# Four indirect transfers under way at most, and rows before weights in the 256-token lists

## The chip, the core and the metric

The kernel runs on one core of one Trainium2 chip. The metric is the device time of one execution in microseconds. Before the change it was 1098.66 us, the median of three runs (1090.99, 1098.66, 1099.57). Five engines work side by side and wait for each other through semaphores: TensorE (PE in the profile; PEld is its weight load), VectorE (DVE), ScalarE (ACT), GpSimd (POOL) and SyncE (SP). In this kernel SP only issues plain and transposing DMAs, and POOL almost only issues indirect ones.

## What is computed

The input `x` has 8 batches of 2496 tokens with 256 channels. A two-dimensional Fourier transform is taken over tokens and channels of each batch and its real part kept. Each of the 19,968 resulting rows then goes through one of 8 experts:

```python
x = np.fft.fft(np.fft.fft(x, axis=1), axis=2).real      # per batch
logits = x @ w_gate + modality_bias[modality_id]
e_idx = np.argmax(logits, axis=1)
gate_w = softmax(logits)[arange(N), e_idx]
for e in range(8):
    mask = e_idx == e
    out[mask] = gate_w[mask, None] * (np.maximum(x[mask] @ w1[e], 0) @ w2[e])
```

`w1[e]` is 256 x 1024 and `w2[e]` is 1024 x 256.

## The kernel before, in words

**Two programs in one.** The stream `Kernel.stream` makes the transform, batch after batch, as matmuls in three stages (lines 517/519, 543 to 552 and 561/563), and routes each batch: for each of its rows it finds the expert and the place in that expert's region of the DRAM buffer `xd`. The expert part `Kernel.block` takes 128 or 256 rows of one expert out of `xd` and runs both layers on them. A driver (`fft_moe`) interleaves the two by the string `SEQ` and later by due times; a scheduler then fixes, when the program is built, the order on every engine from its own idea of when things finish.

**Values are split.** Each fp32 value is held as two fp16 halves, so that a product takes three matmuls (line 1130 for the first layer, L1148 for the second). Before the experts run, the weights are read, split and written to `w16` (lines 881 to 928).

**Scatters.** A batch's rows are written to `xd` by 22 indirect DMAs of GpSimd (`scatter`, L744), each of up to 117 rows of 1032 bytes, from tiles `rp` and `rm`. The next tile `rm` is filled by DVE (L218 to L221) when an earlier scatter from its buffer has landed. There are 3 `rm` buffers early on.

**A block** (`block`). SP reads the block's first row, its expert and a flag from a small table (lines 1101 to 1105, `TENSOR_LOAD`); loads the expert's weights `w1` and `w2` (L1108, L1109; 1 MB each, skipped where the flag says that the slot has them already; three slots); fetches the rows transposed as `xT` (L1114, three buffers); and fetches `ig`, each row's token number and gate (L1117, four buffers). PE makes the first layer (L1130), ACT and DVE bring it out of PSUM as two halves of `H` (L1135, L1136), PE makes the second layer into the only `pso` buffer (L1148), DVE computes the row factor `gs` from `ig` (L1151), ACT scales `pso` into `ob` (L1154, two buffers, one of 128 rows each), and GpSimd writes `ob` to the output rows that `ig` names (L1155, indirect). So a 256-row block has two `ob` and two output transfers.

**Lists.** The first 19 blocks follow a fixed plan, with sizes 128 and 256. Then come six lists of 256-row blocks, one after batch 2 and one after every later batch (5, 10, 9, 10, 10 and 10 blocks), and at the end a list of 128-row blocks.

**Who is kept apart from whom.** Dependences between DMAs that write the same DRAM tensor are declared away: scatters belong to the group `xd_w` and declare no dependence on that group (`scatter_dep`), output transfers do the same with the group `out_w` (L1158, L1159).

**Queues.** SP issues its DMAs in program order: one that waits holds all that stand behind it. So does POOL. The indirect DMAs of POOL take eight completion counters in turn (`DMASW0` to `DMASW7`), and each waits until the transfer that had its counter before, the eighth before it, has landed.

Of the kernel before, what the change touches and what calls it, by code (L numbers as in the profile page):

```python
# [24 lines left out]
E, F = 8, 1024  # L25
# [30 lines left out]
WROW = 8208  # L56
# [34 lines left out]
CUT = 6  # L91
LAG = 1
SM = 3
HA = 0
GROUPS = {0: (1, (128,) * 3 + (0,) * 5), 1: (2, (128,) * 3 + (256,) * 3 + (0,) * 2),
          2: (3, (256,) * 8), 3: (3, (0,) * 6 + (256,) * 2)}
# [140 lines left out]
class Kernel:  # L237
    def __init__(self, ctx, tc, t):
        self.ctx, self.tc, self.nc, self.t = ctx, tc, tc.nc, t
        nc = self.nc  # L240
        pool = lambda name, bufs=1, **k: ctx.enter_context(tc.tile_pool(name=name, bufs=bufs, **k))
        self.cpool = c = pool("consts")
        self.fft = pool("fft", 2)
        self.rt = pool("route", 2)
        self.psf = pool("psf", 4, space=PSUM)
        self.psm = pool("psm", 3, space=PSUM)
        self.pso = pool("pso", 1, space=PSUM)
        self.pool = pool

        self.ready = -1  # L250
        self.parts = 0
        self.head = None
        self.XM = [None, None]

        def const(name, shape, dt=F32):
            x = c.tile(shape, dt, name=name)
            nc.sync.dma_start(x, t["c_" + name])
            return x

        self.load_x(0, 0, 0)  # L260
        self.c1 = c.tile([P, NI, 132], F32, name="c1")
        nc.sync.dma_start(self.c1[:, 0:NH], t["c_c1"][:, 0:NH])
        self.load_x(0, 0, 1)
        if XE:
            self.load_x(0, 1, 0)
            nc.sync.dma_start(self.c1[:, NH:NI], t["c_c1"][:, NH:NI])
            self.load_x(0, 1, 1)
            pk = const("pack", [P, PACK])
        else:
            pk = const("pack", [P, PACK])  # L270
            self.load_x(0, 1, 0)
            nc.sync.dma_start(self.c1[:, NH:NI], t["c_c1"][:, NH:NI])
            self.load_x(0, 1, 1)
        self.mp = pk[:, 0:512].rearrange("p (a c) -> p a c", a=4)
        self.misc = pk[:, 512:584]
        self.pk = pk
        self.wg = pk[:, 584:616].rearrange("p (a c) -> p a c", a=4)
        self.e3 = pk[0:120, 616:616 + 2 * M3].rearrange("p (a c) -> p a c", a=2)
        self.iota = pk[:, 850:978]
        self.ids = const("ids", [M3, B, NC], I32)  # L280
        self.tri = const("tri", [M3, 2, P], F16)
        self.mb = c.tile([P, 2, 8], F32, name="mb")
        nc.sync.dma_start(self.mb, t["mb"].unsqueeze(0).to_broadcast([P, 2, 8]))

        self.ones = c.tile([P, P], F32, name="ones")
        nc.vector.memset(self.ones, 1.0)
        self.base = c.tile([P, 8], F32, name="base")
        nc.vector.tensor_copy(self.base, self.misc[:, 16:24])
        pad = c.tile([P, ROW], I16, name="padrow")
        nc.gpsimd.memset(pad, 0)  # L290
        padi = pad.bitcast(I32)
        nc.gpsimd.memset(padi[:, 256:257], OOB)
        self.padrow = pad
        for i in range(2):
            self.scatter_dep(nc.sync.dma_start(t["xd"][DUMP + i * P: DUMP + (i + 1) * P, :], pad), 0)
        self.done = c.tile([1, 8], F32, name="done0")
        nc.vector.memset(self.done, 0.0)
        self.ntok = 0
        self.extra = 0
        self.ntaken = 0  # L300
        self.nblk = 0
        self.loads = []
        self.pend = []
        self.rows = None
        self.started = False
        self.prev = None
        self.ob = None
        self.off = 0
        self.mark = None
        self.bases = {}  # L310
        self.pos = 0.0
        self.slots = lambda b: 2 * NC
# [430 lines left out]
    def scatter(self, row, at, b):  # L743
        i = self.nc.gpsimd.indirect_dma_start(  # L744
            out=self.t["xd"], out_offset=bass.IndirectOffsetOnAxis(ap=at, axis=0),
            in_=row, in_offset=None, bounds_check=XROWS - 1, oob_is_err=False)
        self.scatter_dep(i, b)
        self.scattered = i.ins

    def drain(self, last):  # L750

# [33 lines left out]
    def stream(self):  # L785
# [13 lines left out]
        for b in range(B):  # L799
# [5 lines left out]
            for g, _ in enumerate(self.stage23(b)):  # L805
# [9 lines left out]
                if b == 0 and g == CUT + LAG - 1:  # L815
                    early = self.route(0, 0, CUT)
                with self.hp(HA):
                    next(early, None)
# [40 lines left out]
    def weights(self, p):  # L859
        U = 2 * E  # L860
        tc = self.tc
        L, A = {}, {}
        for s in range(U + 3):
            if 0 <= s - 3 < U:
                self.wstore(s - 3)
            if s < U:
                L[s] = self.wload(p, s)
            if 0 <= s - LA < U:
                with self.hp(HW), ExitStack() as x:
                    if PS <= s - LA < PS + 2:  # L870
                        x.enter_context(tc.issue_after(self.scattered))
                    A[s - LA] = self.wbound(p, s - LA, L[s - LA])
            if 0 <= s - LA - LB < U:
                with self.hp(HW):
                    self.wsplit(p, s - LA - LB, *A.pop(s - LA - LB))
            yield
# [58 lines left out]
    def first_taken(self):  # L935
        rt, V = self.rt, self.nc.vector
        nd = rt.tile([1, 8], F32, name="sp_d", bufs=2)
        V.memset(nd[:, SM:E], 0.0)
        V.tensor_tensor(nd[:, 0:SM], self.bases[1][0:1, 0:SM], self.misc[0:1, 16:16 + SM], ALU.subtract)
        V.tensor_scalar(nd[:, 0:SM], nd[:, 0:SM], float(P), None, ALU.min)  # L940
        self.done = nd
        self.ntaken += P * SM
        self.extra += SM

# [138 lines left out]
    def block(self, S, ti, i, o=0, n=0, ex=None, load=False, here=False, slot=0):  # L1083

        nc, t, p, tc = self.nc, self.t, self.mo, self.tc
# [4 lines left out]
        first = i < ns  # L1090
        if ex is None:
            w = i % ns
            i = o + sum((n - j + ns - 1) // ns for j in range(w)) + i // ns
        self.nblk += 1
        w1, w2 = self.w1[sl], self.w2[sl]
        kw = {}
        with ExitStack() as st:
# [4 lines left out]
            if ex is None:  # L1102
                ee = nc.sync.value_load(ti[0:1, 1, i:i + 1], min_val=0, max_val=E - 1)
                if not first:
                    kw = dict(cond=nc.sync.value_load(ti[0:1, 2, i:i + 1], min_val=0, max_val=1), cond_hint=False)
        if ex is None or load:
            wsrc = t["w16"][ds(ee, 1)].rearrange("a p f -> (a p) f") if ex is None else t["w16"][ex]
            nc.sync.dma_start(w1, wsrc[:, 0:4 * F], **kw)  # L1108
            nc.sync.dma_start(w2, wsrc[:, 4 * F:WROW], **kw)  # L1109
        if here:  # L1110
            xT, ig = self.onchip(ex)
        else:
            xT = p.tile([P, 4, S], I16, name=f"xT{S}", tag="xT", bufs=3)
            r1 = nc.sync.dma_start_transpose(xT, t["xd"][ds(ro, S), 0:512])  # L1114
            xT = xT.bitcast(F16)
            ig = p.tile([P, NT, 2], F32, name=f"ig{S}", bufs=4)
            r2 = nc.sync.dma_start(ig.bitcast(I16), t["xd"][ds(ro, S), 512:516].rearrange("(t p) c -> p t c", p=P))  # L1117
            self.loads.append(r2.ins)
            self.gather_dep(r1.ins)
            self.gather_dep(r2.ins)  # L1120
        H = p.tile([P, 2, 8, S], F16, name=f"H{S}", tag="H", bufs=2)
        w1v = w1.rearrange("p (h k f) -> p h k f", h=2, k=2)
        NF = 512 // S
        for f0 in range(0, 8, NF):
# [7 lines left out]
            with ExitStack() as st:  # L1132
                if self.ob is not None:
                    st.enter_context(tc.issue_after(self.ob))
                nc.scalar.activation(H[:, 0, f0:f0 + NF, :], ps, AF.Relu)  # L1135
            self.mark = V.scalar_tensor_tensor(H[:, 1, f0:f0 + NF, :], ps, 0.0, H[:, 0, f0:f0 + NF, :], ALU.max, ALU.subtract).ins  # L1136
        self.l1 = l1
# [3 lines left out]
        for tg in range(NT):  # L1141
            k = 0
            for ft in range(8):
                for hh, wh in ((0, 0), (0, 1), (1, 0)):
                    with ExitStack() as st:
                        if S == P and k == 0:
                            st.enter_context(tc.issue_after(self.l1))
                        nc.tensor.matmul(po[:, tg, :], H[:, hh, ft, tg * P:(tg + 1) * P], w2v[:, wh, ft, :], start=k == 0, stop=k == 23)  # L1148
                    k += 1
        gs = p.tile([P, NT], F32, name=f"gs{S}", bufs=3)  # L1150
        V.tensor_scalar(gs, ig[:, :, 1], w2[:, 4 * F:4 * F + 2].bitcast(F32), None, ALU.mult)  # L1151
        for tg in range(NT):
            ob = p.tile([P, D], F32, name="ob", bufs=2)
            self.ob = nc.scalar.activation(ob, po[:, tg, :], AF.Identity, scale=gs[:, tg:tg + 1]).ins  # L1154
            ins = nc.gpsimd.indirect_dma_start(  # L1155
                out=t["out"], out_offset=bass.IndirectOffsetOnAxis(ap=ig.bitcast(I32)[:, tg, 0:1], axis=0),
                in_=ob, in_offset=None, bounds_check=TOK - 1, oob_is_err=False).ins
            tc.declare_no_dep(ins, group="out_w", reason="rows are disjoint")  # L1158
            tc.add_to_no_dep_group("out_w", ins)  # L1159
            if self.started:  # L1160
                self.trickle(ins)
        yield
# [162 lines left out]
```

## Time and profile before

| | before |
|---|---|
| median of the three runs shown | 1098.66 us |
| the profiled execution: device time | 1105.77 us |
| the profiled execution: span of the profile | 1103.9 us |
| PE busy | 1022.9 us |
| POOL busy | 377.4 us |
| DVE, ACT busy | 562.4 us, 442.5 us |
| mean granted TensorE clock | 0.974 |
| mean DMA rate | 213 GB/s |

The span begins at the first instruction and ends with the last; 1.9 us of the device time lie outside it. The profiled execution is 7.1 us longer than the median of the runs. "Busy" adds up the time in which an engine works on at least one instruction. In a row such as `PE psm L1130 <- DVE H L1136` the engine to the left sat idle until the one to the right had finished what stands there; "issue" is idle time for which the profile shows no other engine.

### The profile page before, as it was taken

Reading aid. Unit: us, or ns where it says so; the run is one execution under the profiler, and the core shown is the slowest. Engines: PE = TensorE matmul, PEld = TensorE weight load, DVE = VectorE, ACT = ScalarE, POOL = GpSimd, SP = SyncE. Lnnn points to the kernel's source line nnn. Section 1 sums busy time; section 2 is a strip of 40 time slices with the busy share of each in tenths; the row PEclk is TensorE's granted clock in tenths of the full one; section 3 lists DMA queues with packets and bytes.
Section 4 is the critical chain, followed back from the end, with each engine's and each line's share of the span. In section 5 each row is a group of like instructions: output and inputs, shape, how many; then the busy total and the mean of one; then the engine's idle time right before and its main releaser. Section 6 shows DMA issues by size and latency. Waiting matters only on the chain.

```text
span 1103.9 us, 26274 instructions
## 1 busy us (share of the span) xinstructions
PE 1022.9 (93%) x10069; PEld 916.4 (83%) x10069; DVE 562.4 (51%) x1672; ACT 442.5 (40%) x886; POOL 377.4 (34%) x351
## 2 busy tenths in 40 slices
PE   6789978998897889999999999999999999999996
PEld 5687867987787778989888989887788888889995
DVE  4988866866686565764456434742223222222221
ACT  5667656534434334433343333232223323222331
POOL 0265185134342434324432332344534212211111
PEclk9899988999998899999999999999999999999998
DMA  9388866598377585584966584489678988394963
GB/s 353 150 304 321 264 229 221 159 237 249 128 217 234 184 266 178 148 261 139 287 205 177 163 254 128 111 281 254 191 204 276 261 255 240 95 294 127 267 181 45
DMA packets 151586, 235.56 MB, mean 213 GB/s; under 512 B 115772, under 2 KB 118725, under 8 KB 133533
## 3 DMA queue, kind: packets, MB, share of 16 engines
q1 hardware_dynamic: 132077, 191.65, 59.9%
q0 software_dynamic: 19376, 42.16, 10.8%
q8 instruction: 81, 1.33, 0.5%
q14 instruction: 52, 0.43, 0.1%
HBM read 204.27 MB, written 60.48 MB: 240 GB/s over the span
## 4 chain that ended last, share of the span: by engine, by line
PE 63%; issue 14%; DMA 9%; DVE 4%; POOL 4%; ACT 3%; SPq 2%; another core or an unknown queue 0%; POOLq 0%; DVEq 0%; ACTq 0%
PE pso L1148 28%; PE psm L1130 28%; DMA XM<-x 2%; POOL out L1155 2%; PE psf L561 2%; PE psf L543 2%; POOL xd L744 2%; DMA wa<-w 2%; SPq L1114 2%; DMA out<-ob,ig 1%; PE psf L517 1%; DMA xd<-rm,dsti 1%; ACT wj L896 1%; DMA ig<-xd 1%; DMA c<-c_c 1%
## 5 line engine op out<-in xcount | busy, mean ns | idle before, releaser
L1130 PE MATMUL psm<-xT,w 128*128 128x256 f16 (+1 forms) x4512 | 462.2, 258 | 24.1 <-issue 10.4
L1148 PE MATMUL pso<-w,H 128*128 128x256 f16 x3864 | 459.0, 275 | 11.4 <-issue 10.2
L1130 PEld LDWEIGHTS <-w 128*128 128x128 f16 x4512 | 387.7, 98 | 65.8 <-issue 27.6
L1148 PEld LDWEIGHTS <-H 128*128 128x128 f16 x3864 | 378.0, 99 | 63.0 <-issue 18.3
L1136 DVE SCALAR_TENSOR_TENSOR H<-psm,H 128x512 f16<-128x512 f32 x322 | 218.7, 686 | 298.3 <-ACT H L1135 236.4
L1155 POOL DMA_INDIRECT out<-ob,ig x161 | 162.4, 1009 | 594.2 <-ACT ob L1154 563.0
L1135 ACT ACTIVATE H<-psm 128x512 f16<-128x512 f32 x322 | 189.0, 598 | 298.3 <-PE psm L1130 205.3
L1154 ACT ACTIVATE ob<-pso,gs 128x256 f32<-128x256 f32 x161 | 69.5, 470 | 235.7 <-PE pso L1148 171.8
L744 POOL DMA_INDIRECT xd<-rp,dsti x88 | 102.6, 1166 | 91.2 <-issue 75.3
L744 POOL DMA_INDIRECT xd<-rm,dsti x88 | 103.8, 1180 | 30.7 <-issue 24.1
L498 DVE SCALAR_TENSOR_TENSOR T<-psf,T 120x280 f16<-120x280 f32 (+2 forms) x95 | 43.5, 463 | 56.3 <-ACT T L497 46.4
L1151 DVE TENSOR_SCALAR gs<-ig,w 128x2 f32<-128x2 f32 (+1 forms) x94 | 21.3, 227 | 81.8 <-DMA ig<-xd 65.6
L497 ACT ACTIVATE T<-psf 120x280 f16<-120x280 f32 (+2 forms) x95 | 39.4, 426 | 18.1 <-PE psf L543 8.5
L561 PE MATMUL psf<-T,pack 120*117 120x145 f16 x330 | 35.0, 227 | 9.5 <-DVE T L498 5.3
L896 ACT ACTIVATE wj<-wa 128x1024 f16<-128x1024 f32 x32 | 34.1, 1064 | 15.2 <-DMA wa<-w 15.0
L561 PEld LDWEIGHTS <-pack 120*117 120x117 f16 x330 | 29.2, 135 | 8.8 <-issue 7.7
L379 DVE TENSOR_TENSOR XM<-XM 128x1280 f32<-128x1280 f32 (+2 forms) x18 | 24.1, 1339 | 20.6 <-DMA XM<-x 20.6
L543 PE MATMUL psf<-pack,T 128*120 128x144 f16 x330 | 33.2, 233 | 0.3 <-issue 0.3
L922 DVE SCALAR_TENSOR_TENSOR w<-wa,wsc,w 128x1024 f16<-128x1024 f32 (+1 forms) x16 | 28.9, 1809 | 2.0 <-ACT w L921 1.9
L921 ACT ACTIVATE w<-wa,wsc 128x1024 f16<-128x1024 f32 (+1 forms) x16 | 25.0, 1569 | 10.4 <-DVE w L922 6.2
L382 ACT ACTIVATE XM<-XM 128x1280 f32<-128x1280 f32 x16 | 20.4, 1276 | 21.8 <-DVE XM L379 21.8
L548 PE MATMUL psf<-m2u,T 128*120 128x280 f32 x88 | 28.1, 446 | 1.1 <-DVE Lg L571 0.5
(214 smaller groups left out, 689.7 us busy)
## 6 DMA issues: line engine op xcount, KB each, us to landing
w<-w SPq DMA_DIRECT2D x86, 1028.0 KB
w<-w SPq DMA_DIRECT2D x86, 1024.0 KB
XM<-x SPq DMA_DIRECT2D x14, 1280.0 KB
wa<-w SPq DMA_DIRECT2D x16, 1024.0 KB
out<-ob,ig POOLq DMA_INDIRECT x161
XM<-x SPq DMA_DIRECT2D x2, 768.0 KB
xT<-xd SPq DMA_TRANSPOSE x91
xd<-rp,dsti POOLq DMA_INDIRECT x88
```

What stands on the lines that cost most here:

```text
L497: self.nc.scalar.activation(dst[:, 0], ps, AF.Identity, scale=scale)
L498: self.mark = self.nc.vector.scalar_tensor_tensor(dst[:, 1], ps, scale, dst[:, 0], ALU.mult, ALU.subtract).ins
L543: nc.tensor.matmul(oh, T1[h][:, a, g, :], self.m2h[h][:, w], start=h + k == 0, stop=h * k == 2, skip_group_check=True)
L561: nc.tensor.matmul(ps3[0:M3, cols], self.e3h[:, a, j, :], T2[:, w, cols], start=k == 0, stop=k == 2)
L744: i = self.nc.gpsimd.indirect_dma_start(out=self.t["xd"], out_offset=bass.IndirectOffsetOnAxis(ap=at, axis=0), in_=row, in_offset=None, bo ...
L896: nc.scalar.activation(jk, x, AF.Square, accum_out=st[:, i:i + 1])
L1130: l1 = nc.tensor.matmul(ps[:, q, :], w1v[:, h, kt, ft], xT[:, xs, :], start=k == 0, stop=k == 5).ins
L1135: nc.scalar.activation(H[:, 0, f0:f0 + NF, :], ps, AF.Relu)
L1136: self.mark = V.scalar_tensor_tensor(H[:, 1, f0:f0 + NF, :], ps, 0.0, H[:, 0, f0:f0 + NF, :], ALU.max, ALU.subtract).ins
L1148: nc.tensor.matmul(po[:, tg, :], H[:, hh, ft, tg * P:(tg + 1) * P], w2v[:, wh, ft, :], start=k == 0, stop=k == 23)
L1154: self.ob = nc.scalar.activation(ob, po[:, tg, :], AF.Identity, scale=gs[:, tg:tg + 1]).ins
L1155: ins = nc.gpsimd.indirect_dma_start(out=t["out"], out_offset=bass.IndirectOffsetOnAxis(ap=ig.bitcast(I32)[:, tg, 0:1], axis=0), in_=ob, i ...
```

## The change

It has two parts. `limit` is called for each scatter and each output transfer, in the order in which the program is written, and adds a dependence on the one four places before. In `block`, for blocks of the 256-row lists other than a list's first three, the two weight loads are written after `xT` and `ig` instead of before them.

```diff
+FLIGHT = 4
...
+        self.flight = []
...
         self.scatter_dep(i, b)
         self.scattered = i.ins
+        self.limit(i.ins)
+
+    def limit(self, ins):
+        self.flight.append(ins)
+        if len(self.flight) > FLIGHT:
+            self.tc.add_manual_dep(ins, self.flight[-1 - FLIGHT].name, mybir.DependencyInfo(
+                mybir.DependencyClass.Sync, mybir.DependencyReason.DATA), reason="bounds the scatters under way")
...
-        if ex is None or load:
-            wsrc = t["w16"][ds(ee, 1)].rearrange("a p f -> (a p) f") if ex is None else t["w16"][ex]
-            nc.sync.dma_start(w1, wsrc[:, 0:4 * F], **kw)
-            nc.sync.dma_start(w2, wsrc[:, 4 * F:WROW], **kw)
+        def weights():
+            if ex is None or load:
+                wsrc = t["w16"][ds(ee, 1)].rearrange("a p f -> (a p) f") if ex is None else t["w16"][ex]
+                nc.sync.dma_start(w1, wsrc[:, 0:4 * F], **kw)
+                nc.sync.dma_start(w2, wsrc[:, 4 * F:WROW], **kw)
+
+        ahead = ex is None and not first and S == 256
+        if not ahead:
+            weights()
         if here:
             xT, ig = self.onchip(ex)
         else:
...
+        if ahead:
+            weights()
...
             tc.add_to_no_dep_group("out_w", ins)
+            self.limit(ins)
```

The scheduler turns this into new orders and waits. Three places show it. The first is POOL, at the end of the burst of 12 scatters that opens batch 0, with the first output transfer behind it. Before:

```order
L744 DMA xd<-rm,dsti 162048x516 [waits DMASW1_49]
L744 DMA xd<-rm,dsti 162048x516 [waits DMASW2_49]
L744 DMA xd<-rm,dsti 162048x516 [waits DMASW3_49]
L1155 DMA out<-ob,ig_568 19968x256 [waits DMASW4_49,Activation_49]
L744 DMA xd<-rp,dsti 162048x516 [waits DMASW5_49,DVE_49]
```

Now:

```order
L746 DMA xd<-rm,dsti 162048x516 [waits DMASW1_49]
L746 DMA xd<-rm,dsti 162048x516 [waits DMASW2_49]
L746 DMA xd<-rm,dsti 162048x516 [waits DMASW3_49]
L1171 DMA out<-ob,ig_568 19968x256 [waits DMASW4_49,DMASW0_49,Activation_49]
L746 DMA xd<-rp,dsti 162048x516 [waits DMASW5_49,DVE_49]
```

Only the output transfer has a wait more, for a scatter (`DMASW0`). The scatters wait for the counters that they waited for before, so nothing was added between one scatter and another.

The second place is ACT in batch 2, where the second half of a 256-row block's output (`ob_2272`) stood right behind the first (`ob_2267`). Before:

```order
L1154 ACTIVATE ob_2267<-pso_2216,gs256_2265 128x256 [waits DMASW2_49,PE_49]
L1154 ACTIVATE ob_2272<-pso_2216,gs256_2265 128x256 [waits DMASW7_49]
L896 ACTIVATE wj_2710,wst_2709<-wa_2083 128x1024 [waits Activation_49]
L553 COPY T2_2727<-psf_2726 120x280 [waits PE_49]
L497 ACTIVATE rp_2127<-psf_2731,xsc_1798 117x256 [waits PE_49]
L1135 ACTIVATE H256_2293<-psm_2294 128x512 [waits PE_49]
```

Now:

```order
L1170 ACTIVATE ob_2267<-pso_2216,gs256_2265 128x256 [waits DMASW2_49,PE_49]
L905 ACTIVATE wj_2710,wst_2709<-wa_2083 128x1024 [waits Activation_49]
L555 COPY T2_2727<-psf_2726 120x280 [waits PE_49]
L499 ACTIVATE rp_2127<-psf_2731,xsc_1798 117x256 [waits PE_49]
L1170 ACTIVATE ob_2272<-pso_2216,gs256_2265 128x256 [waits DMASW3_49]
L1151 ACTIVATE H256_2293<-psm_2294 128x512 [waits PE_49]
```

It now stands behind three instructions of the weights and the transform, and the output transfer whose buffer it takes over has the counter `DMASW3` in place of `DMASW7`: on POOL that transfer has gone from the first place behind a burst of 12 scatters to the fifth, behind four scatters of the next `rp` and `rm`.

The third place is SP in the last list of 256-row blocks, from one transposed fetch on. Before:

```order
L1114 DMA_TRANSPOSE xT_12914<-xd 128x4x256 [waits DMAHW1_49,PE_49]
L1109 DMA w_2_109<-w 128x4112 [waits DMAHW2_49,DVE_49,PE_49]
L1117 DMA ig_12755<-xd 128x2x4 [waits DMAHW3_49,DMASW3_49,DMASW0_49]
L1108 DMA w_0_104<-w 128x4096 [waits DMAHW4_49]
...
L1114 DMA_TRANSPOSE xT_13075<-xd 128x4x256 [waits DMAHW5_49,PE_49]
```

Now:

```order
L1128 DMA_TRANSPOSE xT_12912<-xd 128x4x256 [waits DMAHW2_49,PE_49]
...
L1119 DMA w_2_109<-w 128x4112 [waits DMAHW3_49,DVE_49,PE_49]
L1131 DMA ig_12914<-xd 128x2x4 [waits DMAHW4_49,DMASW5_49,DMASW0_49]
L1118 DMA w_0_104<-w 128x4096 [waits DMAHW5_49]
L1128 DMA_TRANSPOSE xT_13073<-xd 128x4x256 [waits DMAHW6_49,PE_49]
```

The fetch of `ig` behind the load of `w2` is now the one of the same block as the `xT` before it; before it was that of the block before. `xT`, `w1` and `w2` keep their order among themselves.

## Rows read from the trace of the kernel before

**Rows 1.** The page: the span, the engines' busy times, and the two DMA queues with data (q1 is SP's, q0 POOL's; packets, MB, share of the time of 16 DMA engines).

```profile
span 1103.9 us, 26274 instructions
...
PE 1022.9 (93%) x10069; PEld 916.4 (83%) x10069; DVE 562.4 (51%) x1672; ACT 442.5 (40%) x886; POOL 377.4 (34%) x351
...
q1 hardware_dynamic: 132077, 191.65, 59.9%
q0 software_dynamic: 19376, 42.16, 10.8%
```

**Rows 2.** Busy time of each engine in six stages: start and end, length, PE, PEld, DVE, ACT and POOL in us with their instructions, the granted clock, the DMA engines' share, GB/s.

```profile
0.00:130.00 130.00, 106.41 (x965) 94.02 (x966) 100.72 (x331) 85.21 (x165) 40.87 (x32) 0.93 0.78 273
130.00:220.00 90.00, 77.67 (x663) 69.02 (x661) 65.13 (x199) 56.08 (x102) 43.87 (x32) 0.92 0.65 216
220.00:440.00 220.00, 197.11 (x1935) 173.69 (x1933) 141.81 (x470) 87.36 (x192) 87.29 (x82) 0.96 0.71 213
440.00:800.00 360.00, 349.69 (x3366) 312.89 (x3365) 174.88 (x529) 124.82 (x265) 137.10 (x135) 1.00 0.69 199
800.00:980.00 180.00, 180.00 (x1673) 161.48 (x1672) 49.48 (x87) 54.48 (x102) 45.90 (x47) 1.00 0.78 226
980.00:1104.00 124.00, 112.05 (x1478) 105.31 (x1475) 30.33 (x59) 34.56 (x63) 22.35 (x23) 0.96 0.66 173
```

**Rows 3.** PE's waits between 130 and 220 us, longest in total first: total us, times, longest.

```profile
PE psm L1130 <- DVE H L1136: 6.4, 1, 6.4
PE psf L563 <- DVE xeb L388: 2.3, 1, 2.3
PE psm L1130 <- issue: 1.7, 1, 1.7
```

**Rows 4.** PE's waits between 440 and 800 us, the longest and the one by another engine's work in the expert part (columns as above).

```profile
PE pso L1148 <- issue: 7.4, 12, 0.9
...
PE psm L1130 <- DVE H L1136: 0.5, 1, 0.5
```

**Rows 5.** Waits of all engines over the whole span, the rows that bear on indirect transfers and on `ig` (columns as above).

```profile
POOL out L1155 <- ACT ob L1154: 563.0, 89, 17.8
...
DVE gs L1151 <- DMA ig<-xd: 65.6, 33, 5.9
...
ACT ob L1154 <- DMA out<-ob,ig: 5.9, 4, 2.5
```

**Rows 6.** Timeline of all engines around 159 to 184 us: start, duration, engine, line, operation, tiles, count, and in brackets the idle time before it and what ended it.

```profile
159.19 0.99 POOL L744 DMA_INDIRECT xd<-rm,dsti  x1 [0.30 <-issue]
160.48 0.99 POOL L1155 DMA_INDIRECT out<-ob,ig  x1 [0.30 <-ACT wj L896]
161.78 1.00 POOL L744 DMA_INDIRECT xd<-rp,dsti  x1 [0.30 <-issue]
...
163.30 0.17 DVE L218 COPY rm<-tail 117x4 int32<-117x4 int32 x1 [10.39 <-DMA xd<-rm,dsti]
...
164.18 0.58 PE L1130 MATMUL psm<-xT,w 128*128 128x256 f16 x2 [6.41 <-DVE H L1136]
...
168.78 1.30 POOL L744 DMA_INDIRECT xd<-rm,dsti  x1 [0.30 <-issue]
...
170.38 0.49 ACT L497 ACTIVATE rp<-psf,xsc 117x256 f16<-117x256 f32 x1
...
171.99 4.42 PE L1148 MATMUL pso<-w,H 128*128 128x256 f16 x39
...
174.58 0.99 POOL L1155 DMA_INDIRECT out<-ob,ig  x1 [0.30 <-issue]
...
182.40 0.47 ACT L1154 ACTIVATE ob<-pso,gs 128x256 f32<-128x256 f32 x1 [2.31 <-DMA out<-ob,ig]
...
183.98 0.71 PE L563 MATMUL psf<-T,pack 120*117 120x145 f32 x4 [2.28 <-DVE xeb L388]
```

**Rows 7.** Timeline of POOL in the last list of 256-row blocks (columns as above): the output transfers of three blocks.

```profile
830.23 0.97 POOL L1155 DMA_INDIRECT out<-ob,ig  x1 [0.30 <-ACT H L1135]
...
838.15 0.97 POOL L1155 DMA_INDIRECT out<-ob,ig  x1 [5.67 <-ACT ob L1154]
...
840.71 0.97 POOL L1155 DMA_INDIRECT out<-ob,ig  x1 [0.31 <-issue]
...
848.63 0.97 POOL L1155 DMA_INDIRECT out<-ob,ig  x1 [5.68 <-ACT ob L1154]
```

**Rows 8.** Timeline of all engines in the same stretch, the ACT instruction that waits for an output transfer (columns as above).

```profile
838.63 0.47 ACT L1154 ACTIVATE ob<-pso,gs 128x256 f32<-128x256 f32 x1 [0.75 <-DMA out<-ob,ig]
```

**Rows 9.** Timeline of SP's queue in the same stretch (columns as above).

```profile
847.83 0.33 SPq L1109 DMA_DIRECT2D w<-w  x1
848.42 0.38 SPq L1117 DMA_DIRECT2D ig<-xd  x1
849.02 0.33 SPq L1108 DMA_DIRECT2D w<-w  x1
```

**Rows 10.** SP's own waits over the whole span: total us, times, longest.

```profile
SPq L1109 <- PE pso L1148: 178.0, 57, 15.8
...
SPq L1117 <- DMA out<-ob,ig: 17.1, 9, 8.7
```

## The prediction

> **What bounds the kernel now.** I read the stages first, then PE's waits in them, then the two queues that the change touches. PE is busy for 1022.9 of 1103.9 us [rows 1]. By stage [rows 2] it leaves idle 130 - 106.4 = 23.6 us before 130 us, 90 - 77.7 = 12.3 us up to 220, 220 - 197.1 = 22.9 us up to 440, 360 - 349.7 = 10.3 us up to 800, nothing up to 980, and 12.0 us at the end, most of it after the last matmul. So from 440 us on PE itself is the bound, and whatever arrives earlier there can give back 10 us at most. From 130 to 440 us PE waits for 35 us, and its granted clock is 0.92 and 0.96, which means that for part of the time it got 1.2 instead of 2.4 GHz: another 0.08 x 90 + 0.04 x 220 = 16 us at most.
>
> What ends the waits matters more than their sum. Between 130 and 220 us they have names [rows 3]: 6.4 us for `H` from DVE, 2.3 us for a scale of the transform. The first is told by the timeline [rows 6]: at 163.30 DVE had stood for 10.39 us at the copy into `rm`, until an earlier scatter from that buffer had landed; `H` stood behind it, and PE, which had waited 6.41 us, went on at 164.18. Between 440 and 800 us hardly any wait is for another engine's work [rows 4].
>
> POOL is no bound: it waits 563 us for `ob` alone [rows 5]. But it is a queue, and its transfers take long to land. Three rows bound that. The last scatter of the burst starts at 159.19 and frees DVE at 163.30, so 4.1 us; the output transfer of 174.58 frees ACT at 182.40, so 7.8 us [rows 6]; the one of 830.23 frees ACT at 838.63, so 8.4 us [rows 7, 8]. In a dense run POOL issues every 1.30 us (159.19, 160.48, 161.78) [rows 6]. Waiting for the fourth before therefore costs between nothing (4.1 is under 4 x 1.30 = 5.2) and 8.4 - 5.2 = 3.2 us.
>
> **Part 1, the limit.** It is weaker than its name. Scatters declare no dependence on scatters, output transfers none on output transfers; an added dependence between two of a kind falls under that, and the orders bear it out: the burst of 12 scatters has the waits that it had. What is left are pairs of a scatter and an output transfer. In the program as built 97 of 379 indirect transfers name a scatter or output transfer three to six places back, where before none did. In runs of one kind, which are the bursts of batch 0 and the lists of 128 rows, nothing is added, and in the lists where the two kinds alternate the fourth before is of the same kind. So the DVE wait of 10.39 us neither goes nor grows: price 0.
>
> For the mixed pairs the price is 0 to 3.2 us each on POOL, and POOL's idle time hides it unless somebody waits for the landing: ACT for an `ob` buffer (before, 5.9 us in 4 waits) or SP for an `ig` buffer (17.1 us in 9) [rows 5, 10]. With four ACT waits growing by 0 to 3.2 us that is 0 to 13 us on ACT, in front of PSUM that has three buffers for the first layer; nearest is the 7.8 us landing, 2.6 us per wait, and since most of these waits lie where PE has other matmuls I put +1.5 us on the path.
>
> The Trainium skill ("DMA: Bandwidth & Descriptors", Anatomy of one DMA) puts such a transfer at about 2.0 us plus its bytes over 436 GB/s, which would be an estimated 2.3 us for a scatter; the limit would then never wait and the 1.5 us would be 0. The trace doesn't agree: 4.1 to 8.4 us.
>
> **Part 2, the order that follows.** The scheduler moves work in batch 2. The output transfer that POOL issued at 160.48 now stands behind four scatters, which took from 161.78 to 168.78, 7.0 us, so it starts at about 167.5. The second half of the next block, `ob_2272`, needs its buffer: with 4.1 us to land that is 171.6, with 7.8 us 175.3. On ACT it follows the `rp` instruction of 170.38 + 0.49 = 170.9. So ACT, and the `H` of the next block behind it, stand for 0.7 to 4.4 us. PE's second layer at 171.99 needs the one `pso` buffer that this `ob` empties. In the new order PE does some of the transform first, so I take the upper landing, 4.4 us, and cover 2 of it: +2.4 us. Against that, the transform's total, for whose result PE waited 2.28 us at 183.98, now comes ahead of that second layer: -2.3 us. The rest of the reordering up to some 220 us interchanges work of equal size. Net 0, bounds -12.3 (all idle time of the stage goes) and +4.4.
>
> **Part 3, rows before weights.** It applies to 36 blocks, 54 less three in each of six lists. What moves in SP's queue is `ig`, by one block. The gain is on DVE, which waits 65.6 us for `ig` [rows 5]; but PE isn't waiting for DVE there [rows 4], so I price it at 0, bounds -10.3 and 0. The cost: `ig` takes a buffer that the outputs of four blocks ago must have left. SP reaches it at 848.42; the second output of that block went out at 840.71 [rows 7, 9] and lands, at 8.4 us, at 849.1. SP stands for 0.7 us and the next `w1` behind it. Blocks follow every 10.48 us (838.15, 848.63) [rows 7], and `w1` is loaded two blocks before its use by the order of the layers, so 21 us cover it: price 0. Were the cover gone, 36 x 0.7 = 25 us.
>
> **Sum.** 0 + 1.5 + 0 + 0 = +1.5 us on the profiled execution's 1105.77 us, that is 1107.3. That execution is 7.1 us above the median of 1098.66; I put the difference on the median: **1100 us**. For this kernel about 1% (11 us) can be told from no change; the three runs alone spread over 8.6 us.
>
> **Rivals.**
>
> *Slower: the late output transfer.* One mechanism, ACT standing at `ob` because the output transfer whose buffer it needs was put back on POOL. In favour: ACT already waits for landings [rows 5]; a stop of 6.41 us on PE stood in the stage with clock 0.92. It decides from where the landing takes over 7 us in stretches with dense scatters. Price: 4.4 us in batch 2, the upper 13 us of the limit on ACT, less the 2.3 us gain: 15, at 1114 us. Against it: `ob` waits were 4 in all. Chance 0.15.
>
> *Faster: the reordering closes the stage.* If the transform's earlier place lets PE run through from 164 to 220 us and the waits and the lower clock there go by two thirds, that is two thirds of 12.3 + 7.2 us, 13 us, at 1086 us. For it: DVE's waits for `ig` also stop. Against: the largest wait, 6.4 us, has its cause on POOL ahead of the changed part. A variant is that fewer indirect transfers leave the weights more of the DMA engines. Against that variant: q0 takes 10.8% of the engines' time beside 59.9% [rows 1], and its bytes stay. By the Trainium skill (same page, Queues, rings and completion order) each engine takes turns between the queues by packets; then a queue with four transfers in hand gets the turns of one with eight, and this variant would give 0. No row here shows the turns. Chance 0.17.
>
> *The limit holds for all pairs.* A burst of 12 would then go at 7.8 us for four instead of 5.2, so 2 x 2.6 = 5.2 us later, in two places: +10 us, 1109. The orders speak against it: 0.02.
>
> The forecast has 0.66. Its own range is 1093 to 1107: the three runs of the same kernel lie up to 7.7 us from their median, and the two priced terms can each be out by 3 or 4 us without one of the rivals. To leave out no more than 2 in 10 I take 1086 to 1112, which cuts about half of the faster case and half of the slower one. Faster by over 1% (under 1087.7) has 0.17, slower by over 1% (over 1109.6) 0.15, the same 0.68: the forecast and the last rival.
>
> **What will show it.** Right, if from 800 to 980 us PE is again busy throughout and DVE's wait for `ig` falls from 65.6 us to under 40 with no gain there; if DVE's wait at `rm` is still near 10 us; and if the scale's 2.3 us are gone from PE's waits while ACT's wait for output transfers has grown above 5.9 us. The first part is wrong if scatters of one burst are spread by more than 1.3 us with no wait of another engine; the third if SP's wait at `ig` reaches PE as a wait of L1130 for `w` or `xT`. The forecast fails if 130 to 440 us change by over 11 us in length for the same matmuls.

## The result and the profile after

The changed kernel takes 1105.18 us (median of 19 runs, 1097.54 to 1118.86), the kernel before, beside it, 1096.1 us (19 runs): a ratio of 1.0092, 95% interval [1.0066, 1.0118]. That is some 10 us slower, inside the 1% that the prediction calls no change and inside its range, but not the 1.5 us that the sum said. Beside the later experiments the change came out at 1.0095. Every ratio is of undisturbed runs alone, so it need not be the quotient of the two medians.

The profiled execution of after takes 1103.82 us with a span of 1102.0, that of before 1105.77 and 1103.9. The one of before was a long one, so the two can't be subtracted; what the change did has to be read from the waits. First all engines' waits in the profile of after: total us, times, longest.

```profile
POOL out L1171 <- ACT ob L1170: 515.9, 86, 13.4
...
DVE gs L1167 <- DMA w<-w: 88.1, 24, 8.1
...
DVE gs L1167 <- DMA ig<-xd: 43.6, 17, 6.2
...
POOL xd L746 <- DMA out<-ob,ig: 14.0, 7, 4.6
...
DVE rm L219 <- DMA xd<-rm,dsti: 10.1, 4, 8.1
...
ACT ob L1170 <- DMA out<-ob,ig: 8.7, 4, 5.2
```

They answer to [rows 5]. `gs` waits less for `ig`, as meant (43.6 instead of 65.6 us). But a new wait has come on the same line, for the weights `w2`: 88.1 us. SP's own waits in the profile of after tell where it comes from; they answer to [rows 10]:

```profile
SPq L1131 <- DMA out<-ob,ig: 207.8, 49, 12.2
SPq L1119 <- PE pso L1164: 80.3, 32, 14.3
```

SP stands at `ig`, until output transfers have landed, for 207.8 us where it was 17.1, and its wait at `w2` for PE has shrunk from 178.0 to 80.3 us: SP now comes to `w2` when PE has long left the buffer. The stages of after, columns as in [rows 2]:

```profile
0.00:130.00 130.00, 107.13 (x968) 94.41 (x969) 101.21 (x333) 86.94 (x167) 40.35 (x32) 0.93 0.80 276
130.00:220.00 90.00, 80.70 (x684) 71.56 (x682) 67.55 (x211) 54.84 (x100) 41.68 (x32) 0.92 0.66 218
220.00:440.00 220.00, 196.10 (x1925) 173.79 (x1923) 140.47 (x457) 88.47 (x193) 86.66 (x83) 0.96 0.69 211
440.00:800.00 360.00, 352.70 (x3405) 317.00 (x3403) 174.85 (x531) 125.83 (x264) 137.92 (x137) 1.00 0.70 201
800.00:980.00 180.00, 176.50 (x1640) 157.82 (x1638) 46.93 (x84) 53.63 (x101) 44.00 (x45) 1.00 0.78 226
```

From 800 to 980 us, where PE had no gap, it now leaves 180 - 176.5 = 3.5 us idle and does 1640 matmuls instead of 1673. PE's waits of after between 130 and 220 us (these answer to [rows 3]), and then its only one from 800 to 980 us:

```profile
PE psm L1146 <- DVE sp_d L974: 4.5, 1, 4.5
PE pso L1164 <- ACT ob L1170: 3.4, 2, 2.4
```

```profile
PE psm L1146 <- DVE H L1152: 3.4, 3, 1.5
```

What stands behind the first two is seen in the timeline of all engines of after in batch 2:

```profile
158.97 0.17 DVE L219 COPY rm<-tail 117x4 int32<-117x4 int32 x1 [8.08 <-DMA xd<-rm,dsti]
...
159.85 0.58 PE L1146 MATMUL psm<-xT,w 128*128 128x256 f16 x2 [4.45 <-DVE sp_d L974]
...
161.42 2.73 POOL L1171 DMA_INDIRECT out<-ob,ig  x1 [0.67 <-issue]
...
171.40 0.47 ACT L1170 ACTIVATE ob<-pso,gs 128x256 f32<-128x256 f32 x1 [5.22 <-DMA out<-ob,ig]
```

The 4.5 us put down to `sp_d` are the stop of [rows 6] again: DVE stood for 8.08 us at the copy into `rm`, `sp_d` comes right behind it, and PE goes on at 159.85. And ACT stands for 5.22 us until the output transfer of 161.42 has landed; PE's 2.4 us at the second layer follow from that.

How the 207.8 us on SP become idle time on PE is seen in the timeline of all engines of after, in the last list of 256-row blocks (start, duration, engine, line, what, and in brackets the idle time before and what ended it):

```profile
832.12 0.33 SPq L1118 DMA_DIRECT2D w<-w  x1
...
832.64 0.97 POOL L1171 DMA_INDIRECT out<-ob,ig  x1 [5.67 <-ACT ob L1170]
...
835.19 0.98 POOL L1171 DMA_INDIRECT out<-ob,ig  x1 [0.30 <-issue]
835.76 0.47 SPq L1119 DMA_DIRECT2D w<-w  x1
...
842.47 0.39 SPq L1131 DMA_DIRECT2D ig<-xd  x1
843.14 0.33 SPq L1118 DMA_DIRECT2D w<-w  x1
...
844.76 0.97 POOL L1171 DMA_INDIRECT out<-ob,ig  x1 [7.31 <-ACT ob L1170]
...
845.56 0.23 DVE L1167 TENSOR_SCALAR gs<-ig,w 128x2 f32<-128x2 f32 x1 [8.14 <-DMA w<-w]
...
845.70 1.88 DVE L1152 SCALAR_TENSOR_TENSOR H<-psm,H 128x512 f16<-128x512 f32 x3
...
846.44 2.78 PE L1146 MATMUL psm<-xT,w 128*128 128x256 f16 x24 [1.21 <-DVE H L1152]
...
866.34 0.84 ACT L1170 ACTIVATE ob<-pso,gs 128x256 f32<-128x256 f32 x2 [3.71 <-PE pso L1164]
```

Read it from the top. SP has issued `w2` at 835.76 and comes to `ig`. The buffer is left by the transfers that POOL issued at 832.64 and 835.19; SP gets on at 842.47, and only then issues `w1` of the next block at 843.14, with its `w2` behind that. DVE meanwhile stands at `gs`, which needs the scale at the end of `w2`: the load of 835.76 lets it go at 845.56. Three evictions to `H` were queued behind and go in one piece, and PE, which needs the PSUM that they empty, has lost 1.21 us. POOL's first output transfers of two blocks follow each other by 844.76 - 832.64 = 12.12 us instead of 10.48 [rows 7].

In the order as built, the `gs` of 845.56 is the one that ACT first reads at 866.34, 20.8 us later. So DVE, whose order is fixed, held up three evictions that PE was waiting for, for a factor that was needed two blocks on. A later place for `gs` on DVE was not tried.

In the same place of the kernel before, on the timeline of all engines:

```profile
828.17 0.33 SPq L1108 DMA_DIRECT2D w<-w  x1
...
837.35 0.35 SPq L1109 DMA_DIRECT2D w<-w  x1
...
843.12 0.23 DVE L1151 TENSOR_SCALAR gs<-ig,w 128x2 f32<-128x2 f32 x1 [1.54 <-DMA w<-w]
...
851.19 0.97 POOL L1155 DMA_INDIRECT out<-ob,ig  x1 [0.30 <-ACT H L1135]
```

There `w2` lands 843.12 - 837.35 = 5.8 us after its issue, with `w1` 837.35 - 828.17 = 9.2 us ahead of it, and DVE stands for 1.54 us. After the change it is 845.56 - 835.76 = 9.8 us: `w1`, held up at `ig`, had gone only 835.76 - 832.12 = 3.6 us ahead. The two halves of a block's weights, which were spread over the block, now follow each other closely. The 9.8 us are near the upper end: of the loads of `w2` that DVE waited for in the whole profile of after, the 12 with `w1` 3.6 to 5.0 us ahead landed 5.8 to 11.3 us after their issue, half of them within 7, and the 5 with `w1` over 9 us ahead after 5.1 to 5.8.

### The profile page after: what moved, and what is told of

It reads as the page before. It is cut to its first block, busy times and chain, and to the rows that moved or that the text cites. A ratio compares the mean times of both kernels' runs of the same rounds, so it can differ in the third digit from the quotient of the medians.

```text
span 1102.0 us, 26294 instructions
## 1 busy us (share of the span) xinstructions
PE 1022.3 (93%) x10069; PEld 916.9 (83%) x10069; DVE 561.3 (51%) x1672; ACT 444.2 (40%) x886; POOL 373.0 (34%) x351
## 4 chain that ended last, share of the span: by engine, by line
PE 55%; issue 16%; DMA 14%; DVE 6%; POOL 3%; SPq 3%; ACT 2%; POOLq 0%; DVEq 0%; ACTq 0%
PE pso L1164 24%; PE psm L1146 24%; DMA XM<-x 3%; DMA w<-w 3%; POOL out L1171 2%; DMA wa<-w 2%; DMA out<-ob,ig 2%; PE psf L545 2%; PE psf L563 2%; SPq L1128 2%; PE psf L550 1%; PE psf L519 1%; POOL xd L746 1%; DVE H L1152 1%; DMA xd<-rp,dsti 1%
## 5 line engine op out<-in xcount | busy, mean ns | idle before, releaser
L1151 ACT ACTIVATE H<-psm 128x512 f16<-128x512 f32 x322 | 189.4, 598 | 280.0 <-PE psm L1146 210.7
L746 POOL DMA_INDIRECT xd<-rp,dsti x88 | 97.5, 1107 | 100.4 <-issue 75.3
L1167 DVE TENSOR_SCALAR gs<-ig,w 128x2 f32<-128x2 f32 (+1 forms) x94 | 21.5, 229 | 144.8 <-DMA w<-w 88.1
L384 ACT ACTIVATE XM<-XM 128x1280 f32<-128x1280 f32 x16 | 20.4, 1276 | 26.9 <-DVE XM L381 26.9
L545 PEld LDWEIGHTS <-T 128*120 128x120 f16 x330 | 28.2, 138 | 2.7 <-issue 2.2
L499 ACT ACTIVATE rp<-psf 117x256 f16<-117x256 f32 x55 | 21.2, 388 | 22.8 <-PE psf L563 9.4
```

Of the source, the lines that this page charges most:

```text
L499: self.nc.scalar.activation(dst[:, 0], ps, AF.Identity, scale=scale)
L545: nc.tensor.matmul(oh, T1[h][:, a, g, :], self.m2h[h][:, w], start=h + k == 0, stop=h * k == 2, skip_group_check=True)
L746: i = self.nc.gpsimd.indirect_dma_start(out=self.t["xd"], out_offset=bass.IndirectOffsetOnAxis(ap=at, axis=0), in_=row, in_offset=None, bo ...
```

## The experiments

Theory A: the loss comes from SP, which stands at `ig` ahead of the weights. Theory B: it comes from the limit on transfers under way. The first four kernels take the two parts apart.

**The limit alone** (`limit` as in the change, weights where they were):

> The limit without the other part. Theory A (the loss comes from SP, which stands at the fetch of ig until the outputs of four blocks ago have landed, with w2 of the next block behind it): ratio to before 0.997 to 1.003, SP's wait at ig for output transfers stays near 17 us, DVE's wait at gs for w stays near 9 us. Theory B (the loss comes from the limit, through output transfers that start later and the order it makes in batch 2): ratio 1.006 to 1.012, with the loss between 130 and 440 us.

Measured: 1100.81 beside 1100.68 us, ratio 1.0003 [0.9968, 1.0038]. SP's waits with the limit alone:

```profile
SPq L1118 <- PE pso L1157: 172.2, 55, 14.5
...
SPq L1126 <- DMA out<-ob,ig: 32.4, 11, 11.1
```

The wait at `ig` is 32.4 us, above the 17 that theory A gave, but far from 207.8. By itself the limit is worth nothing that can be seen (0.4% at most either way), and theory B falls as the whole explanation.

**The order alone** (no calls of `limit`):

> Rows and gates before weights, without the limit. Theory A: ratio 1.006 to 1.012, SP's wait at ig for output transfers over 150 us, DVE's wait at gs for w over 60 us, PE idle by 2 to 5 us between 800 and 980 us. Theory B: ratio 0.997 to 1.003 although those waits are there.

Measured: ratio 1.0045 [1.0014, 1.0076]. SP's wait in this kernel, and DVE's in the view of all waits:

```profile
SPq L1130 <- DMA out<-ob,ig: 191.6, 44, 8.4
```

```profile
DVE gs L1166 <- DMA w<-w: 86.6, 21, 8.0
```

Both waits of the change are there without the limit. The time lost is less than the change's, though, and below theory A's range of 1.006 to 1.012; that question comes back below.

**The change with eight `ig` buffers:**

```diff
-            ig = p.tile([P, NT, 2], F32, name=f"ig{S}", bufs=4)
+            ig = p.tile([P, NT, 2], F32, name=f"ig{S}", bufs=8)
```

(and the same for the 128-row tile made on the chip).

> The whole change, with eight buffers for ig in place of four, so that a fetch of ig waits for outputs of eight blocks ago. Theory A: SP's wait at ig for output transfers falls from 208 us to under 30, DVE's wait at gs for w from 88 to under 20, PE is busy throughout between 800 and 980 us, ratio 0.995 to 1.003. Theory B: the waits fall in the same way, but the ratio stays at 1.006 to 1.012.

Measured: 1100.79 us, ratio 0.9990 [0.9960, 1.0019]; PE is busy throughout from 800 to 980 us. SP's wait, DVE's in the view of all waits, and the stage:

```profile
SPq L1131 <- DMA out<-ob,ig: 9.3, 3, 6.5
```

```profile
DVE gs L1167 <- DMA w<-w: 25.4, 18, 2.6
```

```profile
800.00:980.00 180.00, 180.00 (x1699) 161.88 (x1697) 48.93 (x86) 55.08 (x103) 44.88 (x46) 1.00 0.79 229
```

DVE's wait for `w2` fell from 88.1 to 25.4 us, where under 20 was expected; its longest is 2.6 us, and PE doesn't feel it. The whole loss goes with SP's wait. **The kernel before with eight buffers** shows whether buffers help by themselves:

> The kernel before with eight buffers for ig: what the buffers do by themselves. Both theories: ratio 0.997 to 1.003, since before SP stood only 17 us at ig and PE did not wait for it; SP's wait at ig for output transfers falls to under 5 us.

Measured: ratio 0.9977 [0.9951, 1.0003], SP's wait at `ig` 5.8 us (under 5 was expected). They give nothing that can be told from 0, so the 0.9990 is the change mended and not another gain that hides a loss.

**The change with five buffers** asks how large the shortage is.

> The whole change with five ig buffers instead of four. Theory A: one more buffer gives SP one block more, about 10.5 us, and its mean wait was 4.2 us and the longest 12.2, so the wait falls from 208 to under 40 us and the ratio is 0.997 to 1.004, as with eight buffers (0.999). Rival (the wait is not of one block's size but a backlog that follows any number of buffers): SP's wait stays above 100 us and the ratio above 1.005.

Measured: ratio 1.0011 [0.9982, 1.0041]. SP's wait:

```profile
SPq L1131 <- DMA out<-ob,ig: 27.1, 8, 11.3
```

One buffer does it. The wait was for one block more than there were buffers, not a backlog.

**Only `xT` ahead of the weights:** the two lines that write the weights stand between the fetch of `xT` and that of `ig`.

```diff
+            if ahead:
+                weights()
             ig = p.tile([P, NT, 2], F32, name=f"ig{S}", bufs=4)
...
-        if ahead:
-            weights()
```

> The whole change, but only xT is written ahead of the weights; ig stays behind them, where it was before. Theory A: the harm is ig's place alone, so SP's wait for landed outputs is back at 15 to 35 us, DVE's wait for w under 15 us, ratio 0.997 to 1.003. Rival (putting the transposed fetch ahead of 2 MB of weights costs by itself): ratio above 1.005 with SP's wait for outputs small.

Measured: ratio 1.0021 [0.9993, 1.0050], SP's wait at `ig` 37.5 us in 11, DVE's wait for `w` 4.7 us. The wait is just over the range that theory A gave, the ratio inside. So the harm is `ig`'s place; the transposed fetch may go ahead.

**`gs` on POOL instead of DVE** cuts the chain further down: SP still stands, but nothing on DVE does.

```diff
-        V.tensor_scalar(gs, ig[:, :, 1], w2[:, 4 * F:4 * F + 2].bitcast(F32), None, ALU.mult)
+        nc.gpsimd.tensor_scalar(gs, ig[:, :, 1], w2[:, 4 * F:4 * F + 2].bitcast(F32), None, ALU.mult)
```

> The whole change with four ig buffers, but gs is computed by POOL instead of DVE. Theory A (SP stands at ig, w2 comes late, DVE stands at gs in front of H, and that is how it reaches PE): SP's wait at ig stays near 200 us, but DVE no longer stands for w, PE is busy for 180 us of 800 to 980 again, and the ratio to before is 0.996 to 1.004. If instead late loads reach PE by another way (w1 or xT late for the first layer, w2 late for the second), the ratio stays near 1.009 and PE's waits name w or xT. Third possibility: POOL, standing for w2, sends outputs later, SP's wait grows above 250 us and the time with it.

Measured: ratio 1.0032 [1.0001, 1.0062]. SP's wait, the wait of `gs` (now in POOL's), and the stage from 800 to 980 us:

```profile
SPq L1131 <- DMA out<-ob,ig: 218.3, 47, 8.4
```

```profile
POOL gs L1167 <- DMA w<-w: 77.0, 16, 9.1
```

```profile
800.00:980.00 180.00, 179.54 (x1688) 161.04 (x1686) 45.60 (x67) 54.42 (x102) 51.39 (x65) 1.00 0.77 228
```

SP waits as long as before the edit, the weights are as late, and PE's idle time in the stage is 0.46 us instead of 3.5, none of it a wait for `w` or `xT`. This shows the last link: the late weights reached PE through DVE's queue, where `gs` stands ahead of `H`, and not as late operands of a matmul. The time recovers for the greater part, not wholly; POOL, which stands for `w2` now, is the likely rest (ACT's wait for output transfers went to 21.2 us), but that was not tried apart.

**The change once more**, unaltered, on the chip of the last three kernels below:

> The change itself, unaltered, beside the others on one chip. If the reordering alone explains its loss (measured apart: 1.0045, from 1.0014 to 1.0076), the ratio is 1.004 to 1.008; if the limit adds to it in company (an output transfer that waits for a scatter leaves ig's buffer later), it is again 1.008 to 1.012. SP's wait at ig near 200 us under both.

Measured: ratio 1.0095 [1.0068, 1.0122]; SP's wait at `ig` 210.7 us in 50. With the first measurement that makes 1.0093 +- 0.0019 for both parts, against 1.0045 +- 0.0031 for the order alone: 0.0048 +- 0.0036. Whether the limit costs more in company than alone does not follow, since the limit alone is known only to 0.0035 either way. That it makes an output transfer leave `ig`'s buffer later isn't shown either: SP's longest wait is 12.2 and 11.7 us in the change and 8.4 without the limit, but also 8.4 with `gs` on POOL, where the limit is in. Where these 5 us go stays open.

**A limit that holds for all pairs.** The prediction's last rival was that the limit might bind within bursts too. In the change it doesn't, because the groups declare dependences between two transfers of a kind away. Here each group is cut into four by place, and a transfer declares away all but its own:

```diff
+        n = len(self.flight) % 4
+        for k in range(4):
+            if k != n:
+                tc.declare_no_dep(i, group=f"xdw_{k}", reason="rows are disjoint")
...
-        tc.add_to_no_dep_group("xd_w", i)
+        tc.add_to_no_dep_group(f"xdw_{n}" if len(self.flight) else "xd_w", i)
```

(the same for the output transfers; the group `xd_w` is left to the first transfers, the weights stay where they were before).

> Only the limit, the weights where they were, but with the groups that declare dependences away cut into four by place, so that a transfer depends on the fourth before it also when both are scatters or both are output transfers. The prediction's last rival: bursts of 12 go at 7.8 us for four instead of 5.2, about 10 us more in all, ratio 1.009. If scatters land in about 4.1 us, as the first of the rows had it, four under way keep up with POOL's 1.30 us each and the ratio is 0.997 to 1.004. Under either, bursts of scatters on POOL are to show starts more than 1.30 us apart if the limit binds.

Measured: 1086.02 beside 1093.47 us, ratio 0.9928 [0.9903, 0.9954]. Neither theory had a gain. POOL's waits in this kernel show that the limit binds; the second row, one scatter that waits for another, was 5.7 us in 3 with the limit alone as the change has it:

```profile
POOL xd L750 <- DMA out<-ob,ig: 25.5, 13, 6.1
POOL xd L750 <- DMA xd<-rp,dsti: 16.5, 9, 3.4
```

The burst of 12 scatters that opens batch 0 goes from 47.42 to 69.64 us in this kernel and from 48.64 to 69.08 before: 22.2 us instead of 20.4 from the first start to the last.

**The same in two halves**, to find where the gain is made: for the first 60 transfers as written, and from the 61st on.

```diff
-            if k != n:
+            if k != n or not (len(self.flight) < 60):
```

> The limit that holds for all pairs, but only for the first 60 indirect transfers as written (batches 0 to 2 and their blocks, up to about 210 us); later ones as in the change, weights where they were. Theory C: the 0.7% that the full limit gained come from the burst of batch 2, which it breaks up, so that rm is free in time and neither DVE (10.4 us) nor PE (6.4 us) stands at about 160 us: ratio 0.990 to 0.996. Theory D (fewer transfers in hand help the weight loads of the later lists): ratio 0.998 to 1.002 here.

> The mirror of the run before: the limit holds for all pairs only from the 61st indirect transfer on. Theory C: ratio 0.998 to 1.002, with DVE's wait at rm near 10 us as before. Theory D: ratio 0.990 to 0.996. If both halves gain, the gain is made of parts; if neither, the full limit's 0.9928 came from one order of the work that needs both, and its cause stays open.

Measured: the early half 0.9992 [0.9960, 1.0024], the late half 1081.94 beside 1093.3 us, 0.9861 [0.9807, 0.9915] (6 runs; the quotient of the medians is 0.9896). Theory C, the burst of batch 2, falls: DVE's longest wait at `rm` went from 10.4 to 3.0 us in the early half and nothing came of it. The gain is made later. The stage from 220 to 440 us, first in the early half, then in the late one:

```profile
220.00:440.00 220.00, 199.09 (x1940) 175.61 (x1938) 141.66 (x456) 88.54 (x192) 87.06 (x84) 0.96 0.72 219
```

```profile
220.00:440.00 220.00, 202.80 (x2042) 182.30 (x2040) 146.42 (x477) 91.76 (x202) 90.74 (x86) 0.98 0.71 215
```

In the same 220 us the late half does 102 matmuls more, at 180.00 / 1720 = 0.105 us each (the early half's row from 800 to 980 us) 10.7 of the 13.5 us by which the two spans differ (1094.8 and 1081.3). Of that, 202.80 - 199.09 = 3.7 us are less idle time and an estimated 0.02 x 200 = 4 us the higher granted clock, each 0.01 of it being 2 us. But it was 45 matmuls ahead (984 + 706 against 968 + 677) before 220 us already, where its limit does not yet hold for all pairs, so two executions differ by some 5 us without it. The gain lies behind the first 60 transfers, as theory D had it, and is rather larger than its range; that it is made in this stage is read from one execution of each. Whether theory D's reason is right stays open: the limit made the scheduler put the transfers in another order and made POOL wait, and these runs don't take the two apart.

**Both parts mended:** the limit for all pairs, and `ig` and `xT` ahead of the weights with five buffers.

> Both parts of the change, each mended: the limit holds for all pairs, and ig has five buffers so that its place ahead of the weights holds nobody up. Theory A says that the place then costs nothing and the limit keeps its gain: ratio 0.990 to 0.997, SP's wait at ig under 45 us. If more transfers wait for the fourth before, outputs land later and SP stands at ig again: wait above 100 us, ratio above 1.000.

Measured: 1085.47 us, ratio 0.9953 [0.9925, 0.9980], SP's wait at `ig` 19.7 us. That is half a per cent faster than the kernel before, and no better than the limit without the new order (0.9928 throughout, which it can't be told from, and 0.9861 in its late half). No gain of the new order is to be seen even when it holds nobody up.

## Why the prediction was right in its number and wrong in a step

**The number** lies inside the range because the range is wide. The sum had +1.5 us, and the change costs some 10; the baseline of 1098.66 us, from three runs, was 2.6 us above the 1096.1 of 19.

**What bounds the kernel** held: PE is busy for 1022.3 of 1102.0 us, and what costs time are the waits that reach it.

**Part 1** held for the change as it was built. +1.5 us was the term, the run of the limit alone gave +0.3 us with bounds of -3.5 and +4.2 (0.9968 and 1.0038 of 1100.68). A mixed pair's wait came out at 14.0 / 7 = 2.0 us, inside 0 to 3.2, its longest at 4.6 above. The Trainium skill ("DMA: Bandwidth & Descriptors", Anatomy of one DMA), by whose figures an estimated 2.3 us would have let nobody wait, isn't borne out by these 14.0 us. That pairs of one kind were left out, which was read from the orders, is borne out by the run in which they were not. Whether the limit costs more beside the new order stays open, as said.

One reading under it was wrong. The 4.1 us for a scatter to land go from the one of 159.19 to DVE's restart at 163.30 [rows 6]. But three scatters read a tile `rm`, and the copy at 163.30 waits for the counters `DMASW1` to `DMASW3`, which the scatters of 152.71, 154.01 and 155.30 have (on the timeline of POOL before):

```profile
155.30 1.00 POOL L744 DMA_INDIRECT xd<-rm,dsti  x1 [0.30 <-issue]
```

From this one it is 163.30 - 155.30 = 8.0 us. So all three rows say 7.8 to 8.4 us, and by them waiting for the fourth before would cost an estimated 2.6 to 3.2 us in a dense run, not nothing at the lower end. The term itself took 7.8 us and stands.

**Part 2** held in its terms, one of them by luck. The predicted stop of the second layer for `ob` is there, with 2.4 us as its longest, the size that the term had. But the output transfer behind it started at 161.42 and not at 167.5, and took 171.40 - 161.42 = 10.0 us to let ACT go and not 4.1 to 7.8; the two errors nearly cancel, and ACT stood for 5.22 us, above the 0.7 to 4.4. The scale's 2.3 us are gone. PE's idle time from 130 to 220 us went from 12.3 to 9.3 us, within the bounds of net 0; the stop at `rm` is still in it, with 4.5 us where it was 6.4.

**Part 3 failed**, and the loss is there: it goes when SP no longer stands at `ig` (0.9990 and 1.0011). The step was: "SP reaches it at 848.42; the second output of that block went out at 840.71 [rows 7, 9] and lands, at 8.4 us, at 849.1. SP stands for 0.7 us". It took the outputs of the wrong block, one too early: those that the `ig` of the old order had to wait for at this place, and for them the row shows no stop, since `ig` goes 0.6 us behind `w2` [rows 9]. In front of `ig` SP issues `w2` of a block, and that waits for PE to leave the slot, three blocks before. The `ig` behind it is, after the change, that of the next block, and its buffer is left by the outputs of four blocks before that one: of the very block that PE has just finished. In the trace of before these are the transfers of 848.63 [rows 7] and 851.19 (shown above). At 8.4 us the second lands at 859.6, so SP would have stood for 859.6 - 848.4 = 11.2 us. Measured were 207.8 / 49 = 4.2 us as a mean and 12.2 as the longest, since SP, once late, no longer waits for PE at `w2`. The run with five buffers fits this count: one block more, and the wait is gone.

**The cover** failed too. The text let `w1` be late by up to 21 us, looked for a wait of L1130 for `w` or `xT`, and none came in the lists of 256 rows. It overlooked the third reader: `gs`, on DVE, reads the scale that travels with `w2`, and `H` stands behind it. The prediction's opening had described the same pattern for `rm` [rows 6]. Its "Were the cover gone, 36 x 0.7 = 25 us" rests on the wrong 0.7 us and is no measure of the loss, though the loss lies below it.

**What it said would show it:** PE was not busy throughout from 800 to 980 us, and `ig`'s wait stayed above 40 us by 3.6; those two are the failed part. The scale and ACT's wait (8.7, above 5.9) came as said, and the longest wait at `rm` is 8.1 us where it said near 10. The length from 130 to 440 us held: by 440 us after has done 3577 matmuls and before 3563. The sign for part 1, scatters of a burst over 1.3 us apart with no other engine's wait, decides nothing, since the trace of before has them too (from 53.21 to 55.73 us, 2.5 us).

**The rivals.** The late output transfer is there with its stop of 5.22 us on ACT, but not at the price of 15 us: ACT waited 8.7 us in all, and the limit alone costs nothing that can be seen; the kernel grew slower by another way. The reordering did not close the stage: its granted clock is 0.92 as before. The limit for all pairs was priced at +10 us and measured 7.5 us faster (1086.02 against 1093.47): the price let bursts go at 1.30 us a scatter, which the one that opens batch 0 did not even before, so that it grew by 1.8 us instead of 5.2, and it left out what the changed order gives elsewhere.

In single executions the 10 us can't be found whole. PE's waits for `H` and `gs` come to 6.0 + 0.6 us in the profile of after and to 7.9 + 0.8 in the second one of the change, against 1.0 with five buffers and 2.4 with eight; 3.4 us of them are in the stage from 800 to 980 us. The rest is spread over stages in which two executions of the same kernel differ by as much.

## What to carry to other kernels

Before a load is moved ahead in an in-order queue, name the consumer that frees its buffer, and place that consumer in time beside the instruction that then stands in front of the load; an error of one block turned 0.7 us into 11 here. Follow what is held up to every engine that reads it, the small reads too: a scale of four bytes a partition that rides with a 1 MB load stopped PE through DVE's queue, 20.8 us before it was needed. And look whether a dependence that is added survives those that are declared away: the limit as written bound only mixed pairs and gave nothing that can be seen, while one that bound all pairs gave 0.7%, and 1.0 to 1.4% when left out of the first 60, for a reason that stays open.

## What the runs showed of the hardware

Two loads of 1 MB issued close together land later than the same loads apart: `w2` let DVE go after 5.8 us with `w1` 9.2 us ahead of it and after 9.8 us, near the longest, with `w1` 3.6 us ahead. An indirect transfer released the engine that waited for it 7.8 to 8.4 us after its start in the three rows of before, and after 10.0 us in batch 2 of after. And fewer indirect transfers allowed at a time went with 3.7 us less idle time and a granted clock of 0.98 instead of 0.96 from 220 to 440 us, in one execution of each, though the stop at `rm`, which I had taken for the cost of the bursts, was not what it removed.
